# Moving a 448 KB weight load from behind the first V block to the head of the DMA queue, in a decode-attention kernel on one Trainium2 core

## The chip, the cores and the metric

The kernel runs on one core of a Trainium2 chip. The metric is device time in microseconds (us). The profile's span, from the first to the last instruction, is about 2 us shorter than that time (1264.0 against 1266.1 us in the profiled execution of the kernel before). All runs quoted here are single-core runs that the record marks as fast.

## The reference, cut to what matters

A token vector `x` (448 values) attends over a cache of 65536 positions with 8 key/value heads of width 256, two query heads to each of them. The result is mixed with a small layer-normed MLP.

```
q = x @ wq                                  # wq: 448 x 4096, 3.67 MB
p = softmax(q k^T / 16)                     # k_cache: 8 x 65536 x 256 bf16, 268 MB
o = p v                                     # v_cache: the same size
a = o @ wo                                  # wo: 4096 x 448, 3.67 MB
out = g * a + (1 - g) * mlp(x)              # g = sigmoid(sum(x * gate_w))
```

The K and V caches are 537 MB of the 544 MB that the kernel reads. Every byte is read once.

## The kernel before

The sequence is cut into 32 bodies, four to a head pair (two query heads that share one K/V head). A body takes 8.39 MB of K and 8.39 MB of V. SyncE issues all the large loads on one queue. This is its program:

```python
eng.dma_start(wq_a, ...).then_inc(sem_wq, 16)         # rows of 24 KB per partition, 3072 KB
eng.dma_start(wq_b, ...).then_inc(sem_wq, 16)         # rows of 4 KB, 512 KB
for j in range(NP):                                   # 32 bodies
    if j >= 1:
        eng.wait_ge(sem_tr[NB - 1], BODY * (j - 1) + DC)   # PE transposed half of K of body j-1
    load K of body j          # two halves of 4.19 MB in the first and the last body
    if j == 0:
        eng.wait_ge(s_q, 1)   # the q projection is done: wq lies in V's buffer
        eng.wait_ge(s_hb, 1)
    else:
        eng.wait_ge(sem_pv, j)                        # PE has used V of body j-1
    load V of body j          # four pieces in the last body
    g, m = divmod(j, PPH)
    if m == 0 and g < H - 1:
        if g >= 1:
            eng.wait_ge(s_proj, g)                    # PE is done with the wo of pair g-1
        load wo of head pair g                        # rows of 3.5 KB, 448 KB
eng.wait_ge(s_proj, H - 1)
load wo of the last head pair, in two halves
# ... store the result
```

On PE a body is: transpose K chunk by chunk into PSUM, multiply by q, wait for the exponentials, multiply by V. After four bodies the head pair's output is projected with `wo`. The buffers: K has one and a half blocks, V one, and `wq` lies in V's block.

The softmax here doesn't subtract the row's maximum and nothing guards it: scores larger than these inputs give would overflow.

## Time and profile before

| | before |
|---|---|
| time, median of the first 3 runs | 1266.03 us (1266.0 to 1266.64) |
| span | 1264.0 us |
| read from HBM | 544.22 MB, 431 GB/s |
| PE busy | 73% of the span |
| granted TensorE clock, mean | 0.842 |

The table is read like this. Bytes over span give the rate. The row of the DMA engines' busy share is 9 in 39 of the 40 slices and 8 in the last, and the packets of the queue take 99.7% of the 16 engines' span. So I took 431 GB/s for what the transfers do here, with the bytes setting the time. PE's 73% is an average; it shows that PE isn't the bound, not that PE never makes a transfer wait. The prediction below shows the lines.

### The profile page before, as it was taken

The numbers are of one execution on the slowest core, as the hardware profiler recorded it, in microseconds if no ns is written. First come the engines' busy times: TensorE is split into PE (matmuls) and PEld (weight loads), VectorE is DVE, ScalarE is ACT, GpSimd is POOL, SyncE is SP. The second block draws the span as 40 slices with busy tenths as digits, with TensorE's granted clock in tenths as the row PEclk, the third lists the DMA queues.
The fourth block names the chain that finished last, engine by engine and source line by source line (L and its number), as shares of the span: only waits on it lengthen the run. The fifth ranks groups of instructions, "written<-read, shape, count | busy, mean of one in ns | idle before, by whom it ended". The sixth has DMA issues, their size and how long they took to land.

```text
span 1264.0 us, 38850 instructions
## 1 busy us (share of the span) xinstructions
PE 917.0 (73%) x17114; PEld 868.4 (69%) x17114; DVE 422.5 (33%) x764; ACT 538.2 (43%) x788; POOL 0.9 (0%) x7
## 2 busy tenths in 40 slices
PE   3876678766778667786676876758767688676688
PEld 2766668766677666786666876658766578666687
DVE  2433344333444333443222332323322233332233
ACT  1443345533355433454333553335533355433455
POOL 0000000000000000000000000000000000000000
PEclk9887788787898887987888987889887888877999
DMA  9999999999999999999999999999999999999998
GB/s 411 428 434 436 433 431 431 431 438 431 433 433 433 433 431 438 425 433 440 431 436 429 431 431 433 440 433 433 431 431 431 438 436 433 431 433 431 431 427 367
DMA packets 11623, 544.39 MB, mean 431 GB/s; under 512 B 1369, under 2 KB 1628, under 8 KB 2908
## 3 DMA queue, kind: packets, MB, share of 16 engines
q1 hardware_dynamic: 11522, 544.22, 99.7%
q8 instruction: 8, 0.13, 0.0%
q10 hardware_dynamic: 90, 0.01, 0.0%
q14 instruction: 3, 0.02, 0.0%
HBM read 544.22 MB, written 0.00 MB: 431 GB/s over the span
## 4 chain that ended last, share of the span: by engine, by line
DMA 70%; PE 29%; issue 1%; SPq 0%; DVEq 0%; DVE 0%; ACT 0%; ACTq 0%
DMA kring<-in_A_k_cache_dram 68%; PE kst L298 24%; PE sps L318 4%; DMA wo_sb<-in_A_wo_dram 2%; PE acc L358 0%; SPq L231 0%; SPq L265 0%; SPq L228 0%; SPq L226 0%; PE prj L405 0%; PE acc L347 0%; DVEq L92 0%; DVE out_row L634 0%; ACT pT L658 0%; ACTq L658 0%
## 5 line engine op out<-in xcount | busy, mean ns | idle before, releaser
L298 PE MATMUL kst<-ident,kring 128*128 128x128 f32 x4096 | 563.7, 299 | 304.9 <-DMA kring<-in_A_k_cache_dram 294.1
L669 ACT ACTIVATE ktT<-kst 128x1024 bf16<-128x1024 bf16 x512 | 500.0, 1021 | 667.3 <-PE kst L298 666.5
L298 PEld LDWEIGHTS kst<-ident,kring 128*128 128x128 f32 x4096 | 514.0, 156 | 314.8 <-issue 312.2
L569 DVE COPY ktT<-kst 128x1024 bf16<-128x1024 bf16 x512 | 354.2, 692 | 765.0 <-PE kst L298 742.0
L318 PEld LDWEIGHTS sps<-qcur,ktT 128*128 128x128 bf16 x8192 | 237.8, 96 | 4.1 <-issue 1.6
L318 PE MATMUL sps<-qcur,ktT 128*128 128x2 bf16 x8192 | 236.6, 163 | 1.3 <-issue 1.3
L358 PE MATMUL acc<-vbuf,pT 128*2 128x256 bf16 x4080 | 140.4, 305 | 3.8 <-issue 3.3
L358 PEld LDWEIGHTS acc<-vbuf,pT 128*2 128x2 bf16 x4080 | 105.2, 93 | 30.6 <-issue 3.8
L658 ACT ACTIVATE pT<-sps 128x32 f32 x256 | 51.8, 202 | 16.4 <-PE sps L318 16.4
L347 PE MATMUL acc<-pT,ones_sq 128*128 128x32 bf16 x256 | 11.7, 178 | 12.3 <-ACT pT L658 12.3
L347 PEld LDWEIGHTS acc<-pT,ones_sq 128*128 128x128 bf16 x256 | 8.6, 96 | 15.2 <-ACT pT L658 14.9
L675 ACT ACTIVATE z_b<-z_b 128x448 bf16<-128x448 bf16 x14 | 8.1, 577 | 20.5 <-DVE z_b L556 20.4
L575 DVE COPY accs<-acc 128x288 f32<-128x288 f32 x8 | 3.7, 458 | 38.5 <-PE acc L358 38.5
L394 PEld LDWEIGHTS acc<-sel,accs 128*64 128x64 f32 x112 | 10.8, 214 | 0.9
L394 PE MATMUL acc<-sel,accs 128*64 128x1 f32 x112 | 11.4, 260 | 0.0
L431 PE MATMUL acc<-vbuf 42*128 42x42 bf16 x1 | 0.2, 214 | 8.3 <-DMA b_b<-in_B_b_dram 8.3
L405 PE MATMUL prj<-wo_sb,oTn 128*1 128x112 bf16 x128 | 3.7, 244 | 3.1 <-DVE oTn L600 2.9
L431 PEld LDWEIGHTS acc<-vbuf 42*128 42x128 bf16 x1 | 0.1, 102 | 8.4 <-DMA b_b<-in_B_b_dram 8.4
L562 DVE TENSOR_TENSOR gu<-wtmp,z_b 128x448 bf16<-128x448 bf16 x14 | 5.5, 393 | 1.0
L554 DVE TENSOR_TENSOR z_b<-u_b,wtmp 128x448 bf16<-128x448 bf16 x14 | 5.5, 393 | 1.0
L550 DVE TENSOR_TENSOR z_b<-wtmp,u_b 128x448 bf16<-128x448 bf16 x14 | 5.5, 393 | 1.0
L548 DVE TENSOR_TENSOR wtmp<-u_b 128x448 bf16<-128x448 bf16 x14 | 5.5, 392 | 1.1
(89 smaller groups left out, 82.5 us busy)
## 6 DMA issues: line engine op xcount, KB each, us to landing
kring<-in_A_k_cache_dram SPq DMA_DIRECT2D x4, 4096.0 KB, 24.3
vbuf<-in_A_v_cache_dram SPq DMA_DIRECT2D x1, 6144.0 KB, 25.7
wo_sb<-in_A_wo_dram SPq DMA_DIRECT2D x7, 448.0 KB, 27.6
vbuf<-in_A_wq_dram SPq DMA_DIRECT2D x1, 3072.0 KB, 10.2
vbuf<-in_A_v_cache_dram SPq DMA_DIRECT2D x1, 1024.0 KB, 27.8
vbuf<-in_A_v_cache_dram SPq DMA_DIRECT2D x1, 768.0 KB, 28.9
vbuf<-in_A_wq_dram SPq DMA_DIRECT2D x1, 512.0 KB, 10.9
vbuf<-in_A_v_cache_dram SPq DMA_DIRECT2D x31, 29.7
```

Of the source, the lines that this page charges most:

```text
L298: ins = pe.transpose(kst[:, b, i * P:(i + 1) * P], kring_f[:, at + NT * (k % DC) + 4 * b + i, :], ident[:, :])
L318: ins = pe.matmul(sps[:, par, 2 * nt:2 * nt + 2], ktT[:, par, b, ntl * DH + dj:(ntl + 1) * DH:2], qcur[:, dj, :], start=(dj == 0), stop=(d ...
L347: pe.matmul(acc[:, DENC:SELC], ones_sq[:, :], pT[:, r, :], start=False, stop=(r == BODY - 1), skip_group_check=True)
L358: ins = pe.matmul(acc[o:o + REP, 0:DH], pT[:, r, 2 * nt:2 * nt + 2], vbuf[:, n, :], start=False, stop=False, skip_group_check=True)
L394: ins = pe.matmul(dst[hh * HP:(hh + 1) * HP, i:i + 1], accs[:, i:DH:2 * REP], sel[:, hh:hh + 1], start=False, stop=True, skip_group_check= ...
L548: vec.tensor_tensor(W, U, U, op=ALU.mult)
L550: vec.tensor_tensor(Z, W, U, op=ALU.mult)
L554: vec.tensor_tensor(Z, U, W, op=ALU.add)
L569: vec.tensor_copy(ktT[:, k % KTB, b, :], kst_b[:, b, :]).then_inc(sem_ev[b], 1)
L658: act.activation(pT[:, bass.ds(p0 + k % DC, 1), :].rearrange("p o n -> p (o n)"), sps[:, k % 2, 0:2 * NT], AF.Exp, scale=scale).then_inc(s ...
L669: act.activation(ktT[:, k % KTB, b, :], kst_b[:, b, :], AF.Copy).then_inc(sem_ev[b], 1)
L675: act.activation(z_b[:, :], z_b[:, :], AF.Tanh).then_inc(s_tanh, 1)
```

## The change

The load of the first head pair's `wo` is the first of all. The later ones stay where they were. The intent is to have that load out of the way of K and V.

```diff
         @block.sync
         def _(eng):
+            def load_wo(g):
+                w = A_wo[g * REP * DH:(g + 1) * REP * DH, :]
+                eng.dma_start(wo_rows, w.rearrange("(p i) n -> p (i n)", i=2 * REP)).then_inc(sem_wo, 16)
+
+            load_wo(0)
             eng.dma_start(wq_a.rearrange("p j n -> p (j n)"),
 ...
-                if m == 0 and g < H - 1:
-                    if g >= 1:
-                        eng.wait_ge(s_proj, g)
-                    w = A_wo[g * REP * DH:(g + 1) * REP * DH, :]
-                    eng.dma_start(wo_rows, w.rearrange("(p i) n -> p (i n)", i=2 * REP)).then_inc(sem_wo, 16)
+                if m == 0 and 1 <= g < H - 1:
+                    eng.wait_ge(s_proj, g)
+                    load_wo(g)
```

## The prediction

No term of the sum is cut: 1.06 us taken away behind V, 1.06 us added at the head, a ramp of either sign, together 0, give or take 0.5 us. The 1.06 us and the delays of the steps are estimates, bytes over the page's 433 GB/s. The time before the first packet was measured (issue at 0.74 us, first packet at 1.76 us by the packet records). The "some tenths" of the ramp were worked out from nothing that was measured then; the experiments measure them.

> **What bounds the kernel now.** I read the page first, by 40 slices and by queue. It has a bandwidth row, a row of the mean busy share of the 16 DMA engines, and totals.
>
> ```profile
> span 1264.0 us, 38850 instructions
> PE 917.0 (73%) x17114; PEld 868.4 (69%) x17114; DVE 422.5 (33%) x764; ACT 538.2 (43%) x788; POOL 0.9 (0%) x7
> ...
> DMA  9999999999999999999999999999999999999998
> GB/s 411 428 434 436 433 431 431 431 438 431 433 433 433 433 431 438 425 433 440 431 436 429 431 431 433 440 433 433 431 431 431 438 436 433 431 433 431 431 427 367
> ...
> HBM read 544.22 MB, written 0.00 MB: 431 GB/s over the span
> ```
>
> The reader is to see that no slice but the last leaves the DMA engines idle, that the rate is flat near 433 GB/s, and that no compute engine is over 73% busy. 544.22 MB at 433 GB/s is 1256.9 us of the 1264.0, so about 7 us is everything else: the start before the first packet, the ramp, and the end after the last byte. The transfers set the time, and both kernels read the same bytes.
>
> Next I asked what the DMA queue does at the start, because the change touches only that. The timeline of SyncE's queue (start us, us that the issue took, line, destination<-source):
>
> ```profile
> 0.74 0.41 SPq L226 DMA_DIRECT2D vbuf<-in_A_wq_dram  x1
> 1.20 0.41 SPq L228 DMA_DIRECT2D vbuf<-in_A_wq_dram  x1
> 1.67 1.10 SPq L231 DMA_DIRECT2D kring<-in_A_k_cache_dram  x2
> 17.54 0.33 SPq L231 DMA_DIRECT2D vbuf<-in_A_v_cache_dram  x1
> 17.91 0.43 SPq L260 DMA_DIRECT2D wo_sb<-in_A_wo_dram  x1
> 38.79 0.33 SPq L231 DMA_DIRECT2D kring<-in_A_k_cache_dram  x1
> 63.58 0.33 SPq L231 DMA_DIRECT2D vbuf<-in_A_v_cache_dram  x1
> 83.77 0.33 SPq L231 DMA_DIRECT2D kring<-in_A_k_cache_dram  x1
> ```
>
> The issue is a moment and the data come far later. The issues of that same stretch, with KB of each and us from issue to landing (the first 60 us alone):
>
> ```profile
> vbuf<-in_A_wq_dram SPq DMA_DIRECT2D x1, 3072.0 KB, 10.2
> vbuf<-in_A_wq_dram SPq DMA_DIRECT2D x1, 512.0 KB, 10.9
> wo_sb<-in_A_wo_dram SPq DMA_DIRECT2D x1, 448.0 KB, 35.6
> ...
> vbuf<-in_A_v_cache_dram SPq DMA_DIRECT2D x1, 34.8
> kring<-in_A_k_cache_dram SPq DMA_DIRECT2D x1, 34.1
> ```
>
> A transfer of 8.39 MB takes 8.39 / 0.433 = 19.4 us at the flat rate, but V of body 0 lands 34.8 us after its issue: it stood behind others for some 15 us. That backlog is the slack of the queue. Last, windows over the stretch that the change rearranges (columns end with DMA share and GB/s):
>
> ```profile
> 3.00:12.00 9.00, 0.21 (x1) 0.10 (x1) 3.32 (x11) 1.28 (x1) 0.00 (x0) 1.00 1.00 424
> 12.00:32.00 20.00, 9.28 (x154) 8.46 (x155) 4.03 (x17) 3.60 (x5) 0.00 (x0) 1.00 1.03 442
> 32.00:52.00 20.00, 18.66 (x357) 18.30 (x356) 11.47 (x20) 14.45 (x22) 0.00 (x0) 1.00 1.00 430
> 52.00:72.00 20.00, 8.03 (x153) 4.75 (x150) 1.55 (x6) 0.77 (x2) 0.00 (x0) 0.61 1.01 430
> ```
>
> The DMA share is 1.00 or above from 3 us on, although PE does almost nothing before 12 us and is idle for over half of 52 to 72 us. There is no hole for the change to close.
>
> [...] wo, issued at 17.91, lands at 17.91 + 35.6 = 53.5 us, just after V (17.54 + 34.8 = 52.3). [...] Here 0.41 us of issue stands against a landing after 10.2 us.
>
> **The change part by part.**
> Removed: one issue of 0.43 us behind V of body 0, with its 448 KB, which is 0.459 MB / 0.433 = 1.06 us of all the engines. Added: the same transfer at the head of the queue, 1.06 us. The layout and the packets are the same, so the sum over the queue is 0. The branch for later head pairs issues the same loads after the same waits.
> Moved, step by step:
> Step 1. wo is issued at 0.74, wq at 1.20 and 1.66, K at 2.1. Issues follow each other every 0.46 us and the wo data take 1.06 us, so wq's descriptors are there before wo has drained: no bubble.
> Step 2. wq lands 1.06 us later: the later of its two parts from 1.20 + 10.9 = 12.1 to 13.2 us. The projection of q then ends a microsecond later, and V of body 0, which waits for it (and for hbT), is issued at about 18.6 in place of 17.54. By then wq and K of body 0 are queued: 3.67 + 8.39 = 12.06 MB, 27.9 us of engine time from some 1.8 us on, plus 1.06 of wo now. K drains until about 29.7 before and 30.7 after (the landing by the trace is nearer 32). Slack of V's issue: over 12 us before and after. Nothing is lost.
> Step 3. K of body 1 is issued when four of body 0's chunks are transposed, at 38.79 before, at most about 40 after. V then has until 52 us to drain (53.5 with wo behind it before; 53.4 with wo ahead of it after). Slack 13 us or more. What has to be moved before K of body 1 can start is the same bytes in either order, so K of body 1 lands at 38.79 + 34.1 = 72.9 us in both.
> Step 4. V of body 0 itself lands 1.06 us later, 53.4 in place of 52.3, as it now has wo ahead of it. The value matmuls of body 0 began at 53.0 and may slip by about a microsecond; V of body 1 is then issued at 64.6 at the latest in place of 63.58. K of body 1 drains until about 72, so 7 us of slack are left. From K of body 1 on the two kernels have the same schedule.
> Step 5. The first reader of this wo is the projection of head pair 0, at 181.0 us by the view of the wo tile. It was there 127 us early and will be there 177 us early. Nothing is gained on that side.
> What is not balanced is the ramp. The page's first slice moved 411 GB/s in place of 433: 5% of 31.6 us, 1.6 us, is most of it the time before the first packet. Whether short rows (3.5 KB a partition of wo) or long ones (24 KB of wq) meet the first latency could move this by some tenths of a microsecond either way.
> Sum: 0, give or take 0.5 us.
>
> **The rivals.**
> *The delay goes through.* If the q projection stood on the path that sets the end, its 1.06 us would show whole: 1267.1 us. For it: the chain of waits begins with a DMA of K and goes on to PE. Against: every SyncE issue in the table lies 7 to 15 us ahead of the moment at which the engines run dry, and the DMA share has no gap behind it. Even this rival is under 0.1%.
> *The head start pays.* If taking wo from between V of body 0 and K of body 1 brought K forward for good, and the slot at the front were empty time, 1.06 us would be won: 1265.0. For it: the first packets come when the engines are empty. Against: 424 GB/s from 3 to 12 us show no empty time to fill, and wq was issued in the very slot that wo takes.
> *A starved queue.* A later wq shifts all of body 0's work on PE; if one of the issues came after the backlog was gone, the engines would idle by the excess. For this the shift would have to be over 7 us; it is 1.06. PE does stand still for reasons of its own early on ("issue" for 4.34 us before the first K transposes, in the chain of waits), and if those stretches moved unluckily I could lose a few microseconds of slack, still not all. If all of it went wrong, some 3 us: 1269.
>
> **Range and chances.** The three runs before lie within 0.64 us. All rivals together lie between 1265.0 and 1269. I predict 1266.1, with a range of 1265.0 to 1267.5: a microsecond down for the head start, one up for the delay, and a little for scatter. 2% would be 25 us, for which the change has no term: 98.4% within, 0.8% on either side for a state of the chip that I don't see.
>
> **What would show each step right or wrong.** Right: wo issued at 0.74 us and landed by 4; wq's later part landed near 13.2; V of body 0 issued near 18.6; K of body 1 issued at 39 to 41 and landed within 0.7 us of 72.9; the DMA row all 9 and 431 GB/s over the span; the projection of head pair 0 within 0.7 us of 181.0; span 1264 give or take 1. Step 1 is wrong if the first 12 us move fewer bytes than before by more than 0.3 MB; steps 2 to 4 are wrong if the windows between 12 and 92 us show a DMA share under 0.95. The prediction as a whole fails if K of body 1 lands over 1.5 us later than before, or if the rate in the later slices changes[...].

## The result, and the profile after

In runs on the same chip the changed kernel took 1265.7 us (median of 6, 1265.5 to 1266.21) against 1266.1 us (median of 6, 1265.96 to 1266.64). The ratio is 0.9997 with a 95% interval of 0.9984 to 1.001: the same. A ratio is the mean time of one kernel's fast runs over that of the other's in the same rounds, so it is not quite the ratio of the medians quoted.

The page of the changed kernel, the same rows as before:

```profile
span 1263.6 us, 38848 instructions
...
DMA  9999999999999999999999999999999999999998
GB/s 416 430 430 432 434 432 434 436 434 436 432 434 432 432 434 436 425 436 436 438 432 429 432 432 434 436 436 434 432 434 432 440 434 432 432 434 434 432 426 369
...
HBM read 544.22 MB, written 0.00 MB: 431 GB/s over the span
```

The bytes, the rate and the full DMA row are as before. The timeline of SyncE's queue (start, us of the issue, line, what):

```profile
0.74 0.41 SPq L228 DMA_DIRECT2D wo_sb<-in_A_wo_dram  x1
1.20 0.41 SPq L231 DMA_DIRECT2D vbuf<-in_A_wq_dram  x1
1.67 0.43 SPq L233 DMA_DIRECT2D vbuf<-in_A_wq_dram  x1
2.13 1.00 SPq L236 DMA_DIRECT2D kring<-in_A_k_cache_dram  x2
17.85 0.33 SPq L236 DMA_DIRECT2D vbuf<-in_A_v_cache_dram  x1
39.33 0.33 SPq L236 DMA_DIRECT2D kring<-in_A_k_cache_dram  x1
63.58 0.33 SPq L236 DMA_DIRECT2D vbuf<-in_A_v_cache_dram  x1
```

`wo` took the first slot. V of body 0 is issued 0.31 us later than before and K of body 1 0.54 us later; V of body 1 is issued at the same 63.58 (probably by chance: see the end of the section on the backlog). The issues of the first 60 us, KB each and us to landing:

```profile
vbuf<-in_A_wq_dram SPq DMA_DIRECT2D x1, 512.0 KB, 11.1
wo_sb<-in_A_wo_dram SPq DMA_DIRECT2D x1, 448.0 KB, 3.3
...
vbuf<-in_A_v_cache_dram SPq DMA_DIRECT2D x1, 35.3
kring<-in_A_k_cache_dram SPq DMA_DIRECT2D x1, 33.1
```

`wo` lands at 0.74 + 3.3 = 4.0 us and not at 53.5. The second part of `wq` lands at 1.67 + 11.1 = 12.8 us, V of body 0 at 17.85 + 35.3 = 53.2 in place of 52.3, and K of body 1 at 72.5 in place of 72.9. The windows of before, now:

```profile
3.00:12.00 9.00, 0.21 (x1) 0.10 (x1) 3.00 (x11) 1.28 (x1) 0.00 (x0) 1.00 1.02 424
12.00:32.00 20.00, 8.22 (x149) 7.42 (x150) 4.34 (x17) 2.71 (x4) 0.00 (x0) 1.00 1.09 466
32.00:52.00 20.00, 18.86 (x348) 18.50 (x347) 11.09 (x18) 15.13 (x21) 0.00 (x0) 1.00 0.97 414
52.00:72.00 20.00, 8.42 (x167) 5.14 (x163) 1.93 (x8) 0.97 (x3) 0.00 (x0) 0.61 1.02 435
```

A window counts a big packet whole, so the shares of 1.09 and 0.97 to either side of 32 us are to be taken together; there is no hole. Last, two lines of the chain of waits (start, us, what) of the kernel before, then the same two of the changed one:

```profile
38.79 34.06 DMA kring<-in_A_k_cache_dram
...
1232.11 29.33 DMA wo_sb<-in_A_wo_dram
```

```profile
39.33 33.13 DMA kring<-in_A_k_cache_dram
...
1231.94 29.18 DMA wo_sb<-in_A_wo_dram
```

Start plus duration is the landing. K of body 1: 72.85 and 72.46, so 0.39 us earlier. The last load of the program: 1261.44 and 1261.12, 0.32 us earlier. The whole of the small difference is there by 72 us and is carried nearly unchanged to the end.

So two questions were left. Is the 0.4 us real, and does it come from *where* `wo` now stands, or from *what kind of transfer comes first*? And is the reason given for "the same" (a backlog that absorbs a later `wq`) right, and how far does it reach?

### The profile page after: what moved, and what is told of

It reads as the page before. It is cut to its first block, busy times and chain, and to the rows that moved or that the text cites. A ratio compares the mean times of both kernels' runs of the same rounds, so it can differ in the third digit from the quotient of the medians.

```text
span 1263.6 us, 38848 instructions
## 1 busy us (share of the span) xinstructions
PE 920.2 (73%) x17112; PEld 864.9 (68%) x17114; DVE 422.5 (33%) x764; ACT 536.8 (42%) x788; POOL 0.9 (0%) x7
## 4 chain that ended last, share of the span: by engine, by line
DMA 71%; PE 28%; issue 1%; SPq 0%; DVEq 0%; DVE 0%; ACT 0%; ACTq 0%
DMA kring<-in_A_k_cache_dram 68%; PE kst L301 23%; PE sps L321 4%; DMA wo_sb<-in_A_wo_dram 2%; PE acc L361 0%; SPq L236 0%; SPq L233 0%; SPq L268 0%; SPq L231 0%; SPq L228 0%; PE acc L350 0%; DVEq L92 0%; PE prj L408 0%; DVE out_row L637 0%; ACT pT L661 0%
## 5 line engine op out<-in xcount | busy, mean ns | idle before, releaser
L301 PE MATMUL kst<-ident,kring 128*128 128x128 f32 x4096 | 554.2, 296 | 301.5 <-DMA kring<-in_A_k_cache_dram 289.8
L301 PEld LDWEIGHTS kst<-ident,kring 128*128 128x128 f32 x4096 | 504.3, 154 | 311.4 <-issue 308.8
L361 PE MATMUL acc<-vbuf,pT 128*2 128x256 bf16 x4080 | 153.7, 323 | 3.4 <-issue 2.9
L361 PEld LDWEIGHTS acc<-vbuf,pT 128*2 128x2 bf16 x4080 | 111.5, 98 | 37.3 <-issue 3.4
L661 ACT ACTIVATE pT<-sps 128x32 f32 x256 | 52.3, 204 | 16.2 <-PE sps L321 16.2
L350 PE MATMUL acc<-pT,ones_sq 128*128 128x32 bf16 x256 | 11.7, 178 | 12.2 <-ACT pT L661 12.2
## 6 DMA issues: line engine op xcount, KB each, us to landing
vbuf<-in_A_wq_dram SPq DMA_DIRECT2D x1, 512.0 KB, 11.1
```

What stands on the lines that cost most here:

```text
L301: ins = pe.transpose(kst[:, b, i * P:(i + 1) * P], kring_f[:, at + NT * (k % DC) + 4 * b + i, :], ident[:, :])
L350: pe.matmul(acc[:, DENC:SELC], ones_sq[:, :], pT[:, r, :], start=False, stop=(r == BODY - 1), skip_group_check=True)
L361: ins = pe.matmul(acc[o:o + REP, 0:DH], pT[:, r, 2 * nt:2 * nt + 2], vbuf[:, n, :], start=False, stop=False, skip_group_check=True)
L661: act.activation(pT[:, bass.ds(p0 + k % DC, 1), :].rearrange("p o n -> p (o n)"), sps[:, k % 2, 0:2 * NT], AF.Exp, scale=scale).then_inc(s ...
```

## The experiments

### Four orders of the same bytes

**after_again** is the change, unaltered, in the same rounds as its variants.

> The change as it is, once more, to have it on the same chip and rounds as its variants. My theory (the queue is always full, only bytes and the ramp at the start count): 1265.5 to 1265.9 us, 0.2 to 0.6 below the kernel before, because the first packets are 3.5 KB and not 24 KB and so the engines lose less while the first data are under way; wq's second part lands 12.8 us after the start of the span and not 13.2. Rival (the 0.4 us of the first comparison are scatter): within 0.1 us of the kernel before, to either side.

**wo_second** puts `wo` behind `wq`, so that long rows come first again:

```diff
-            load_wo(0)
             eng.dma_start(wq_a ...)
             eng.dma_start(wq_b ...)
+            load_wo(0)
```

> wo of head pair 0 stands behind both parts of wq and ahead of K, so the first packets are the 24 KB rows of wq again. If the small gain comes from short first rows (my theory), it is gone: the time of the kernel before, within 0.15 us, and wq lands at 12.1 us as before. If it comes from taking wo out from between V and K of the first bodies (the head-start rival), it stays: 0.3 to 0.5 us below the kernel before.

**wqb_first** leaves `wo` where it was in the kernel before and only exchanges the two parts of `wq`:

```diff
-            eng.dma_start(wq_a ...)     # rows of 24 KB
             eng.dma_start(wq_b ...)     # rows of 4 KB
+            eng.dma_start(wq_a ...)
```

> The kernel before with the two parts of wq exchanged: the one with 4 KB rows goes first, wo stays behind V. My theory (short first rows): 0.2 to 0.5 us below the kernel before, although wo has not moved at all. Head-start rival: no difference, within 0.15 us.

**wo_late** issues this `wo` only behind V of body 2:

```diff
-                if m == 0 and g < H - 1:
+                if g < H - 1 and m == (0 if g else 2):
```

> wo of head pair 0 is issued behind V of body 2, at about 102 us, and so lands some 30 us later, near 132. Its reader starts at 181. Full-queue theory: the time of the kernel before within 0.2 us; nothing sees the place of this load. If the early place of wo were worth something to its reader, this would be slower than the kernel before by what the landing misses, which is nothing as long as it lands before 181 us.

Measured, five rounds each, against nine runs of the kernel before (1266.07 us, 1265.93 to 1266.55):

| run | first rows | place of wo | time, us | range, us | all of wq landed, us | the same less the bytes ahead of it |
|---|---|---|---|---|---|---|
| before (its profile) | 24 KB | behind V of body 0 | 1266.07 | 1265.93 to 1266.55 | 12.1 | 12.1 |
| wo_second | 24 KB | behind wq | 1266.03 | 1265.78 to 1266.34 | 12.4 | 12.4 |
| wo_late | 24 KB | behind V of body 2 | 1266.08 | 1265.88 to 1266.6 | 12.2 | 12.2 |
| after_again | 3.5 KB | first | 1265.57 | 1265.47 to 1265.64 | 12.7 | 11.6 |
| wqb_first | 4 KB | behind V of body 0 | 1265.58 | 1265.51 to 1265.78 | 11.6 | 11.6 |

The last column takes off 1.06 us where `wo` (0.459 MB at 433 GB/s) runs ahead of `wq`. The landing is read from two views: issue time from the timeline, us to landing from the issues. For wqb_first, whose parts are issued at 0.74 (4 KB rows) and 1.20 us (24 KB rows), the issues say:

```profile
vbuf<-in_A_wq_dram SPq DMA_DIRECT2D x1, 3072.0 KB, 10.4
vbuf<-in_A_wq_dram SPq DMA_DIRECT2D x1, 512.0 KB, 3.3
```

The later landing is 1.20 + 10.4 = 11.6 us, half a microsecond ahead of before although the same bytes were moved from an idle start. For wo_second the 512 KB part is issued at 1.20:

```profile
vbuf<-in_A_wq_dram SPq DMA_DIRECT2D x1, 3072.0 KB, 10.4
vbuf<-in_A_wq_dram SPq DMA_DIRECT2D x1, 512.0 KB, 11.2
```

That is 12.4 us, no gain, with `wo` just as much out of the way of K and V as in the changed kernel.

What follows: the place of `wo` is worth nothing. It may stand first, third or behind 54 MB of other loads, where it lands at 101.48 + 29.6 = 131 us for a reader that starts at 182, and among these orders only which transfer comes first made a difference. Whether it is the length of its rows or its size (448 or 512 KB against 3072 KB) these runs do not separate. Two orders with short first rows took 1265.57 and 1265.58, three with 24 KB first rows 1266.03 to 1266.08. The ten runs of the one kind (1265.47 to 1265.78) lie below the nine of before without overlap; wo_second's fastest, 1265.78, touches them, and in the first comparison two of six runs of the change (1265.99 and 1266.21) lay among those of before. The 95% intervals of the ratios (0.9981 to 1.0009 for after_again) are wider than the effect and do not exclude 1, so half a microsecond rests on the order of the runs and on the landings, not on the ratio.

The packet records of the traces (start, duration and size of every packet, which no view prints one by one) show where about half of it arises. In the kernel before, the first 16 packets of the queue took 1.65 us on average where later ones of the same 24 KB took 0.91. In the changed kernel the first 16, of 3.5 KB, took 0.37 where later ones took 0.14, and in wqb_first 0.34 where later 4 KB packets took 0.16. Summed over every packet that started in the first 6 us and divided by 16 engines, the time beyond the usual is 0.76 us before, 0.73 in wo_second and 0.69 in wo_late, but 0.50 in the profile of the changed kernel, 0.39 in after_again and 0.35 in wqb_first. Why short rows lose less at a cold start no run shows. It is not simply that less is better: a run below with 32 KB first rows had 0.64. This mean over the engines is some 0.3 us lower with short first rows. Another 0.2 us shows at the end, where the engines finish more evenly: their idle time after 1240 us was 3.87, 4.04 and 3.97 us with 24 KB first rows (before, wo_second, wo_late) and 3.69, 3.76 and 3.70 without (the changed kernel, after_again, wqb_first).

### How far the backlog reaches

**wq_mid** issues the first half of K of body 0 ahead of `wq` (the same bytes; `wq` stands behind 4.19 MB more, 9.7 us at 433 GB/s):

```diff
-            eng.dma_start(wq_a ...)
-            eng.dma_start(wq_b ...)
 ...
                     load(kring, A_k_cache, j, HV, NV, 0, sem_k)
+                    eng.dma_start(wq_a ...)
+                    eng.dma_start(wq_b ...)
                     load(kring, A_k_cache, j, 0, HV, 0, sem_kb)
```

> The kernel before with the first half of K of body 0 (4.19 MB, 9.7 us of the engines) ahead of wq. Slack theory: V of body 0 is issued near 27.3 us and not 17.5, and K and wq have drained by about 31.5, so 4 us of slack are left and the time is that of the kernel before within 0.6 us. Delay rival (the q projection stands on the path that sets the end): 9.7 us longer, 1275.8.

**wq_last** puts both halves of K ahead of `wq`:

```diff
-            eng.dma_start(wq_a ...)
-            eng.dma_start(wq_b ...)
 ...
                     load(kring, A_k_cache, j, HV, NV, 0, sem_k)
                     load(kring, A_k_cache, j, 0, HV, 0, sem_kb)
+                    eng.dma_start(wq_a ...)
+                    eng.dma_start(wq_b ...)
```

> The kernel before with all of K of body 0 ahead of wq. Now wq is the last thing in the queue: it lands near 32 us, the projection of q takes 5.4 us more until V of body 0 may be issued (12.1 to 17.5 us in the profile before), and the engines stand idle meanwhile, plus a new first latency of about 1 us. Slack theory: 5 to 7.5 us longer, 1271 to 1273.5, with a hole in the DMA row of that length near 32 to 38 us and nowhere else. Delay rival: 19.4 us longer, 1285. If the backlog later makes up for a hole: as before.

Measured in three rounds beside 1265.99 us (9 runs) of the kernel before: wq_mid 1267.77 us (median of 4, 1266.86 to 1269.01), ratio 1.0017; wq_last 1275.55 us (median of 4, 1275.18 to 1276.2), ratio 1.0077.

The delay rival is out: it wanted 1275.8 and 1285. But my own expectations missed too, by over a microsecond in the first and by two in the second, and for one reason. In wq_mid, V of body 0 was issued at 26.47 us, in time as reckoned. SyncE's timeline shows the issue that came too close, V of body 1:

```profile
69.95 0.33 SPq L227 DMA_DIRECT2D vbuf<-in_A_v_cache_dram  x1
```

It came at 69.95 in place of 63.58 us, because it waits for PE to end body 0, and PE began body 0 some 8 us later. K of body 1 landed at 72.5 us (issued at 47.36, 25.1 to landing). The engines don't end together, and those that were done first had nothing to do. The window just after (DMA share and GB/s last; a window counts a packet whole where it starts, and in the changed kernel the same one shows 0.76 and 328):

```profile
72.00:74.00 2.00, 0.34 (x5) 0.18 (x6) 0.00 (x0) 0.00 (x0) 0.00 (x0) 0.50 0.40 164
```

The profiled execution, at 1266.86 us, is the mildest of the four; the others lost more.

In wq_last the hole that was expected is there:

```profile
31.00:36.00 5.00, 4.31 (x131) 3.77 (x131) 0.91 (x4) 0.00 (x0) 0.00 (x0) 1.00 0.01 3
36.00:37.00 1.00, 0.36 (x1) 0.10 (x1) 0.14 (x1) 0.00 (x0) 0.00 (x0) 1.00 0.00 0
37.00:38.00 1.00, 0.00 (x0) 0.00 (x0) 0.00 (x0) 0.00 (x0) 0.00 (x0) 1.00 2.94 983
```

From 31 to 37 us next to nothing moves (3 and 0 GB/s) while PE projects q. V of body 0 is issued at 36.23 us, and its first packets start in the window from 37. By the packet records, idle engine time up to the end of the hole rose by 6.4 us over that of the kernel before. It rose by 0.9 us between 63 and 95 us, where V of body 1 came at 77.87 us and K of body 1 landed at 80.0: the same second shortage as in wq_mid. Another 0.6 us is elsewhere, most of it at the end, where the engines finish less evenly. Each time the engines had run dry, the next packets took longer than usual again, by 0.6 and 0.7 us per engine, as at the start of the program (which was 0.1 us cheaper here than before, so 1.2 us net). 6.4 + 0.9 + 0.6 + 1.2 = 9.1 us, and the span grew from 1264.0 to 1273.1.

**wq_quarter** tests that reading with a delay that should just fit: a quarter of K ahead of `wq`, on a semaphore of its own, for which PE waits before the q projection.

```diff
-            eng.dma_start(wq_a ...)
-            eng.dma_start(wq_b ...)
 ...
+                    load(kring, A_k_cache, j, HV, HV + 32, 0, sem_kq)
+                    eng.dma_start(wq_a ...)
+                    eng.dma_start(wq_b ...)
-                    load(kring, A_k_cache, j, HV, NV, 0, sem_k)
+                    load(kring, A_k_cache, j, HV + 32, NV, 0, sem_k)
```

> As the run with half of K of body 0 ahead of wq, but with a quarter of it (2.1 MB, 4.84 us of the engines). That run lost 0.9 to 3 us although V of body 0 was issued in time; its trace has a dip of the DMA share at 72 to 74 us, just after V of body 1 was issued at 69.95 us. Theory now: the tightest slack is that of V of body 1, which waits for PE to end body 0, and not that of V of body 0. With 4.84 us of delay V of body 1 should be issued at 66 to 68.5 us, K of body 1 drains at 71 to 72, so no dip: 1265.6 to 1266.4 us, the kernel before within 0.4. Rival (every delay of the q projection costs something like a fifth of itself, as 1.8 us of 9.7): 1267.

It took 1265.96 us (median of 5) against 1266.03, and its five runs range from 1265.59 to 1267.7. In the profiled one V of body 1 was issued at 68.58 us, and by the packet records idle engine time between 63 and 95 us was 0.13 us, against 0.12 before and 0.58 in wq_mid. So by its median a delay of 4.84 us is absorbed and one of 9.7 is not, with the tightest place at V of body 1. (V of body 0 was issued 4.0 us later than before in the one and 8.9 us in the other.) The expectation held for the median but not for every execution: two of the five lost 0.7 and 1.7 us.

"Absorbed" does not mean that it cost nothing. In the profiled execution the packets that started between 68 and 76 us took 0.41 us per engine longer than usual, against 0.04 before and 0.49 in wq_mid. Half of that came back at the start, where its first rows, of 16 KB, lost 0.54 us in place of 0.76.

PE ends body 0 at varying times: V of body 1 was issued between 59.68 and 63.58 us in the traces of the five orders above. So the edge is blurred, and near it the time scatters before its median moves. The traces hold a coincidence in time, which no experiment tested. In its first pass through a body PE stops where the profile names nothing that it waits for, as here in the kernel before, 3.33 us in the middle of the values of body 0:

```profile
58.21 5.33 PE L358 MATMUL acc<-vbuf,pT 128*2 128x256 bf16 x99 [3.33 <-issue]
```

Beside the queues of the loads the page lists one that it calls `q8 instruction`, with 8 packets and 0.13 MB; by the packet records of the kernel before they are of 16 KB each and start between 18.7 and 70.5 us. PE's first transposes start 2.67 to 2.85 us after the second of them starts in all eleven traces, whether that packet starts at 24.12 us (after_again) or at 40.66 (wq_last). The stop shown ends 2.4 us after the sixth, at 55.78. In the changed kernel the sixth starts at 55.73 and PE goes on at 58.19, in place of 58.21: so V of body 1 is issued at the same 63.58 although the values of body 0 began 0.37 us later. In after_again it starts at 53.13, the stop lasts 0.73 us and V of body 1 is issued at 59.68. So the stops before the first transposes and in the values of body 0 move with the packets of that queue. That the one causes the other was not shown.

### Bytes, and the one place where order counts

**extra_bytes** adds to the change a load of 1.835 MB that nothing reads:

```diff
             load_wo(0)
+            eng.dma_start(more[:, :], A_wo[0:8 * DH, :].rearrange("(p i) n -> p (i n)", p=P)
+                          ).then_inc(sem_more, 16)
```

> The change plus a load that nobody reads, 1.835 MB of wo into a tile of its own, right behind wo of head pair 0 (four times the size of the load that the change moves). Full-queue theory: every byte that is added costs its own time wherever it stands, 1.835 / 0.433 = 4.2 us, so 1269.6 to 1270.2. Rival (the front of the queue is empty time that a load may fill for nothing): under 1 us longer.

1269.91 us (median of 4, 1269.77 to 1270.03), which is 4.3 us over after_again (in other rounds; the kernel before took 1265.99 in these), for 4.2 expected. The front of the queue was no free space: the added bytes cost their own time there.

**tail_early** takes the change and moves the *last* head pair's `wo` (again 448 KB) ahead of the last V:

```diff
+                if last:
+                    eng.wait_ge(s_proj, H - 1)
+                    # both halves of the last head pair's wo
                 load(vbuf, A_v_cache, j, 0, NFIRST if last else NV, 0, sem_v)
 ...
-            eng.wait_ge(s_proj, H - 1)
-            # both halves of the last head pair's wo
```

> The change, and besides the last head pair's two loads of wo (448 KB together, as large as the load that the change moves) are taken from the end of the queue to a place ahead of the last V. The bytes are the same, but here the last landing releases work. In the changed kernel the last V piece lands 0.6 us before oTn is done and wo's last part lands last, 0.3 us before the projection ends. With V last, its late values, oTn and all 16 projections follow the last landing: 0.4 to 1.0 us longer than the changed kernel by my reckoning. A theory by which only bytes count, also at the end: no difference within 0.2 us.

1266.31 us (median of 5, 1266.2 to 1267.14), 0.7 us over after_again, which ran in other rounds. The last piece of V lands at 1260.97 us. The end of the chain of waits shows what PE still has to do around and after that:

```profile
1260.45 0.93 PE sps L383 x32
...
1261.40 0.17 DVE oTn L592
...
1261.62 0.40 PE prj L409 x16
```

The last of the late values, the normalisation and all 16 projections follow the landing and end at 1262.02, 1.05 us after it. In the changed kernel `wo` lands last, at 1261.12, and only 8 projections (0.30 us) follow, to 1261.46. The same 448 KB moved at the front were worth nothing by their place; at the end their place is worth 0.7 us, because there a landing releases work and nothing stands behind it to hide that.

No order that was tried beats the changed kernel. wqb_first equals it with a smaller edit.

## Why the prediction was right

The prediction of 1266.1 us (1265.0 to 1267.5) held: 1265.7 us, and 1265.57 in the second set.

- **What bounds.** The bytes do. extra_bytes paid 4.3 us for 1.835 MB, and the rate is 431 GB/s in both kernels.
- **Step 1** (no bubble at the front) held: `wo` landed at 4.0 us, as stated, and the first 12 us moved 0.09 MB less than before (343 against 351 GB/s), where over 0.3 MB was to show it wrong. By the packet records 14 to 17 packets of the queue were under way at every tenth of a microsecond from 2.3 to 7.9 us, so `wo` left no gap behind it.
- **Step 2** ended where it said, with nothing lost, but not for its reasons. A size was off: `wq` landed at 12.8 us and not at 13.2, because the ramp had been set at some tenths of a microsecond "either way" and so at zero in the sum, and it is a gain. By the landings of `wq`, short first rows save 0.4 to 0.5 us; the prediction could not tell the sign because the profile before shows only one kind of first row. And the path was wrong: in the kernel before the q projection does not wait for `wq`. This is its first product, half a microsecond after the landing of `wq` at 12.1:

```profile
12.59 0.24 PE L441 MATMUL sps<-xcol,vbuf 128*128 128x1 bf16 x3 [1.30 <-DVE xcol L517]
```

  It waits 1.30 us for VectorE to make `xcol`, which stands behind small loads on ScalarE's queue: by the profile VectorE's operation L511, ahead of it on that engine, waited 5.10 us for the last of them, `b_b`, until 11.05 us. `xcol` was ready at 12.53 us before and at 12.85 in the changed kernel, where `wq` landed at 12.79, nearly at the same time; and so V of body 0 moved by 0.31 us and not by 1.06. In wqb_first `wq` landed at 11.6, earlier than before, and V of body 0 was issued later, at 18.04. The profile names `wq` as what the first product waits for only in wq_mid (5.9 us), wq_last (14.6 us) and extra_bytes (6.9 us), where more stands ahead of it. In wq_quarter PE stands at this place for 3.9 us and the profile names nothing; that it is `wq` there too is the author's estimate, as 4.84 us more stand ahead of it.
- **Step 3** held: K of body 1 was issued at 39.33 and landed at 72.46, within 0.7 us of the 72.9 stated.
- **Step 4** held for the change: V of body 0 landed at 53.2 (53.4 stated) and V of body 1 was issued at 63.58, no later than before, the second probably by chance (see the stops of PE above). Its "7 us of slack" named the right issue but is a microsecond or two too much. V of body 1 came 6.4 us later than before in the profile of wq_mid, and engines were idle; it came 5.0 us later in that of wq_quarter, and the packets took 0.41 us longer. My expectations for wq_mid and wq_last took the slack of V of body 0 alone and missed for that reason.
- **Step 5** held: the projection of head pair 0 began at 180.8 us, and wo_late shows that even 131 us is early enough for its load.
- **The rivals.** *The delay goes through* is refuted: wq_mid would have cost 9.7 us and cost 1.8. *The head start pays* had the right sign (1265.0), but its mechanism fell: wo_second has the head start and not the gain, wqb_first the gain and not the head start. *A starved queue* does not happen in the change. It does happen in wq_last, with the hole where it was expected.
- **The number.** That the gain of 0.4 to 0.5 us stayed inside the sum's 0.5 us "give or take" is luck: that margin was for a ramp of unknown sign. One reading of the page was also loose: 433 GB/s is not in most slices; 14 of the 40 show 431 and 11 show 433.

## What to carry to other kernels

Here the transfers set the time, and moving a load changed nothing by its place as long as the queue did not run dry (`wo` behind `wq` or behind V of body 2: 1266.03 and 1266.08 us against 1266.07). Before trying such a move, work out for each issue how long the engines still have work after it, and take the tightest of them, not the first. Here `wq` behind 4.84 us of other transfers (their bytes over 433 GB/s) cost nothing in the median, behind 9.7 us 1.8 us, and behind 19.4 us 9.6 us, and the tightest issue was V of body 1, not V of body 0. Check by the waits what really releases each issue: here the load that was to delay V of body 0 was not what V waited for. Order counted where the queue was empty: at the end, where a landing releases work (0.7 us in tail_early), and at the start, where the kind of the first transfer was worth half a microsecond (1265.57 and 1265.58 us against 1266.07). If an execution loses time now and then while the median stands, as in wq_quarter (0.7 and 1.7 us in two of five), look for an issue whose slack is nearly used up.
